# A score tile of four banks with one merge, and fold steps spread, in a kernel of window attention, a Fourier mix and a feed-forward layer

## The chip, the cores and the metric

The kernel runs on one core of a Trainium2 chip, and the metric is the device time of one execution in microseconds (us). The core has five engines that each work off their own queue in order: TensorE (PE, matmuls and transpositions; its weight loads stand in the profile as PEld), VectorE (DVE), ScalarE (ACT), GpSimd (POOL) and SyncE (SP, which here only issues transfers). They meet through semaphores. Matmuls write to PSUM, which has eight banks of 512 fp32 values per partition; the other working memory is SBUF.

## The reference

Attention for 4 batches, 8 heads, 768 positions and a head dimension of 64, with a window of 128 keys and 4 sink keys, then a Fourier mix with a feed-forward layer on the joined heads (width 512, hidden width 2048), all in fp32:

```python
scores = scale * np.matmul(q, k.transpose(0, 1, 3, 2))
keep = is_sink | in_window
scores = np.where(keep, scores, -1000000000.0)
scores = scores - np.max(scores, axis=-1, keepdims=True)
a = np.exp(scores)
a = a / (np.sum(a, axis=-1, keepdims=True) + 1e-09)
x = np.matmul(a, v)                      # then heads side by side: (4, 768, 512)
mixed = np.real(np.fft.fft(np.fft.fft(x, axis=1), axis=2))
u = x + mixed
un = (u - mean(u)) / np.sqrt(var(u) + 1e-06)
out = u + np.maximum(un @ w_ch1, 0.0) @ w_ch2
```

## The kernel before

**Blocks and steps.** Attention works through 24 blocks of 128 queries (4 batches of 6 blocks, numbered 0 to 23 below). A block has four steps, one for each pair of heads; step `s` is block `s // 4`, pair `s % 4`. The order of the instructions is written out by hand: for every step the lists in `SCHEDULE` say in which order ScalarE, VectorE, GpSimd and TensorE get their operations, and this order is kept up to step 97. An operation that belongs to a pair is issued some steps later than its scores (`STEP_LAG`), one that belongs to a block at a step counted from the block's first (`BLOCK_AT`). At an even step `scores` (L694) is called for two pairs, this one and the next: in what follows these four heads are a run, and a block has a first and a second run.

**Scores.** For each head `scores` puts 260 columns into one bank of a tile `s` of two banks (one pair of heads): 128 scores against the older key block, 4 against the sink keys, 128 against the newer block. The pool `ps_s` has two such tiles (L640), so four banks in all; the first pair of a run takes the one, the second the other. In the first block of a batch (blocks 0, 6, 12, 18) there is no older key block, and only 132 columns are written (L700).

**Merge and softs.** Each row needs only 128 of the 256 window scores, some from the older block and some from the newer. `merge` (L704) copies the older block's where the mask `older` says so, over the newer block's, for the two heads of a tile (L708, 128x256). `soft1` (L710) then does, for each head, one VectorE instruction that scales, adds the mask, writes 132 values to SBUF and keeps the row's extreme (L720), followed by a short read of the accumulator. `expo` (L723) is ScalarE's exponential.

**The sink strip.** `trans_sink` (L805, matmul L809) transposes the small sink weights of the block two before. It has no PSUM of its own for that: it writes into columns 384 to 511 of the second bank of the tile that holds the second pair of the current block (`st["free", g + 2, 1][:, 1, 384:]`). It is issued at the block's first step, on TensorE's queue, and `copy_sink` (L812, L814) takes it out with ScalarE at the second step, ahead of the exponentials of that step.

In program order, at the first step of block `g`, VectorE has `merge` and `soft1` of the first pair; then TensorE has the weighted sums of an earlier block (`av`, L789), `trans_sink`, the transpositions of exponentials (`trans_p`, L751), the Fourier matmuls if any (events `T`), and `turn_x` (L801, L803). At the second step ScalarE has `copy_sink`, and VectorE the merge and softs of the second pair, then `store_x` (L819). At the third and fourth step come the second run's. `inverse` (L742, L743) is at the fourth.

**Fourier transform.** `fourier` (L332) is called for a batch when its fourth block has been stored; it registers events by step and engine with `at`. For each of three pairs of 128-row tiles `j` (at `FOLD_AT` = 0, 4, 8 steps): `fold_n` (L351) adds and subtracts mirrored tiles, the sum on VectorE and the difference on GpSimd (`FOLD_ENG`), `fold_m` folds the columns (L361 on VectorE, L358 on GpSimd), `fold_hi` rounds on ScalarE (L364) and `fold_lo` keeps the rest on VectorE (L367). `put_row` (L380), `mid_sum` (L371) and `mid_row` (L375, L377) treat one odd row on VectorE. Then come the matmuls of the transform on TensorE (L394, L421, L442), their rounding on ScalarE (L401, L430) and VectorE (L409, L447, L448) and the update of `u` (L458, L459). The transforms of batches 0 to 2 in the order of work run beside the attention of the next batch; that of the last (`tail`) runs after it, beside the feed-forward layer's first group, and has all its folds on VectorE. The steps are constants:

```python
F_N, F_M, F_S, ROW = (3, 3), (4, 5), (6, 7), (5, 8, 10)
```

**Feed-forward.** From about 203 us weights are converted on VectorE (L590 to L592), split on ScalarE and GpSimd, and used in matmuls L619 and L1124, which fill TensorE to the end.

Of the kernel before, what the change touches and what calls it, by code (L numbers as in the profile page):

```python
# [11 lines left out]
F32 = mybir.dt.float32  # L12
# [7 lines left out]
P = 128  # L20
# [40 lines left out]
FILL_AT, FILL = (24, 36), 0  # L61
FOLD_AT, FOLD_LAST, FOLD_ENG = (0, 4, 8), (0, 4, 8), "VG"

F_N, F_M, F_S, ROW = (3, 3), (4, 5), (6, 7), (5, 8, 10)
EV_A = 0

SINK0_AT = 3, 3, "V"
# [138 lines left out]
def kernel(  # L206
# [63 lines left out]
    def run(general):  # L270
        tag = "g" if general else ""
        with ExitStack() as p1:
# [8 lines left out]
            def at(s, eng, fn):  # L281
                ev.setdefault((s, eng), []).append(fn)
# [49 lines left out]
            def fourier(b, at, ready):  # L332
# [15 lines left out]
                def fold_n(eng, j, odd):  # L348
                    t = fw.tile([P, DM], F32, tag=f"f{odd}", name=f"f{odd}_{b}_{j}", bufs=2 - odd)
                    t_["eo", j, odd] = t  # L350
                    eng.tensor_tensor(t, u[j], u[NHALF + j], op=ALU.subtract if odd else ALU.add)  # L351
# [11 lines left out]
                def fold_hi(j):  # L363
                    A.copy(gh[:, j], t_["g", j])  # L364

                def fold_lo(j):
                    V.tensor_tensor(gl[:, j], t_.pop(("g", j)), f32(gh[:, j]), op=ALU.subtract)  # L367
# [2 lines left out]
                    r = t_["x0"]  # L370
                    V.tensor_tensor(r[:, 1:256], r[:, 1:256], r[:, 511:256:-1], op=ALU.add)  # L371

                def mid_row():
                    t = t_["x0"]
                    V.tensor_copy(sph[:NR, :257], t[:, :257])  # L375
                    lo = sph[NR - 1:NR, :257]
                    V.tensor_tensor(lo, t[NR - 1:NR, :257], f32(lo), op=ALU.subtract)  # L377

# [85 lines left out]
                at(1, "S", load_row)  # L464
                for j in range(NHALF):
                    k = ready[j]
                    e0, e1 = FOLD_TAIL if tail else FOLD_ENG
                    eng = {"V": V, "G": G}
                    at(k + F_N[0], e0, lambda j=j: fold_n(eng[e0], j, 0))
                    at(k + F_N[1], e1, lambda j=j: fold_n(eng[e1], j, 1))  # L470
                    at(k + F_M[0], e0, lambda j=j: fold_m(eng[e0], j, 0))
                    at(k + F_M[1], e1, lambda j=j: fold_m(eng[e1], j, 1))
                    at(k + F_S[0], "A", lambda j=j: fold_hi(j))
                    at(k + F_S[1], "V", lambda j=j: fold_lo(j))
# [160 lines left out]
            def window_attention(fourier, load_constants):  # L635
                with ExitStack() as pa:
                    kpool = pa.enter_context(tc.tile_pool(name="kpool", bufs=1, side="right"))
                    aw = pa.enter_context(tc.tile_pool(name="aw", bufs=2, side="right"))
                    pb = ExitStack()
                    ps_s = pb.enter_context(tc.tile_pool(name="ps_s", bufs=2, space=PSUM))  # L640
                    ps_t = pa.enter_context(tc.tile_pool(name="ps_t", bufs=1, space=PSUM, side="right"))
                    ring = ring_.rearrange("p (h s w) -> p h s w", h=NP, s=NSLOT)
                    ident_r = kpool.tile([P, P], F32R, name="ident_r")
# [48 lines left out]
                        return bass.AP(a.tensor, a.offset, [list(a.ap[0]), [(r1 - r0) * W - 2, 2], [1, W - 2]])  # L692

                    def scores(g, hp):  # L694
                        st["s", g, hp] = st["free", g, hp] = ps = ps_s.tile([P, 2, 512], F32, tag="s", name=f"s_{g}_{hp}")
                        for j in range(2):
                            rows = slice(D * j, D * j + D)
                            if g % NB == 0:
                                q, k = st["whole", g]
                                T.matmul(ps[:, j, P:P + W], q[rows, hp, :], k[rows, hp, :W], start=True, stop=True)  # L700
                            else:
                                T.matmul(ps[:, j, :P + W], st["q", g][rows, hp, :], keys(g, 2 * hp + j), start=True, stop=True)  # L702

                    def merge(g, hp):  # L704
                        ps = st["s", g, hp]
                        qi = g % NB
                        if qi > 0:
                            V.copy_predicated(ps[:, :, P + NS:P + W], older[qi > 2], ps[:, :, 0:P])  # L708

                    def soft1(g, hp):  # L710
# [116 lines left out]
                    with ExitStack() as man:  # L827
# [52 lines left out]
                        V.scalar_tensor_tensor(mask[0][:, 0:1], sdist[:, 0:1], win_ap, nosink[:, 0:1], op0=ALU.is_ge, op1=ALU.mult)  # L880
                        def other_masks():
                            for i, op in enumerate((ALU.is_gt, ALU.is_lt)):
                                V.tensor_scalar(older[i], dist[:, None, :].broadcast_to([P, 2, P]), 0.0, None, op0=op)
# [453 lines left out]
```

## Time and profile before

| what | us |
|---|---|
| median of 3 runs | 786.71 (786.69 to 786.85) |
| the profiled execution | 786.78 |
| its span on the core | 784.9 |
| TensorE busy in the span | 755.2 |
| VectorE busy in the span | 460.6 |
| ScalarE, GpSimd busy | 239.0, 177.6 |

A row of the timeline has the start and the duration in us, engine, line, operation, output and inputs by the program's names, shapes and count, and in brackets how long the engine was idle before it and what ended the wait. A row of the waits has who waited for whom, total, times and longest. A row of groups has line, engine, operation, operands, count, busy time, mean duration in ns, and idle time before with what ended it. A row of stretches has its limits, its length, the busy time of TensorE, its weight loads, VectorE, ScalarE and GpSimd with their counts, TensorE's granted clock, the share of the transfer engines and GB/s.

### The profile page before, as it was taken

The numbers are of one execution on the slowest core, as the hardware profiler recorded it, in microseconds if no ns is written. First come the engines' busy times: TensorE is split into PE (matmuls) and PEld (weight loads), VectorE is DVE, ScalarE is ACT, GpSimd is POOL, SyncE is SP. The second block draws the span as 40 slices with busy tenths as digits, with TensorE's granted clock in tenths as the row PEclk, the third lists the DMA queues.
The fourth block names the chain that finished last, engine by engine and source line by source line (L and its number), as shares of the span: only waits on it lengthen the run. The fifth ranks groups of instructions, "written<-read, shape, count | busy, mean of one in ns | idle before, by whom it ended". The sixth has DMA issues, their size and how long they took to land.

```text
span 784.9 us, 11953 instructions
## 1 busy us (share of the span) xinstructions
PE 755.2 (96%) x4379; PEld 615.8 (78%) x4379; DVE 460.6 (59%) x1354; ACT 239.0 (30%) x704; POOL 177.6 (23%) x283
## 2 busy tenths in 40 slices
PE   7999998988899999999999999999999999999996
PEld 5666876866778878899888888888888888888895
DVE  6788687999999589561356424662456425611211
ACT  4887765756633133221111111111111110110110
POOL 2566477476645255200000000000000000000000
PEclk9999999999999999999999999999999999999999
DMA  9853525433305366120100002000200001000100
GB/s 311 251 171 109 140 84 176 127 112 99 131 27 159 111 196 210 62 71 1 54 1 0 1 9 99 1 1 0 81 1 0 1 0 54 1 1 0 55 1 32
DMA packets 41812, 57.69 MB, mean 74 GB/s; under 512 B 2796, under 2 KB 27500, under 8 KB 41360
## 3 DMA queue, kind: packets, MB, share of 16 engines
q1 hardware_dynamic: 41456, 53.07, 21.7%
q0 software_dynamic: 288, 3.76, 1.2%
q8 instruction: 37, 0.61, 0.3%
q14 instruction: 31, 0.25, 0.1%
HBM read 47.37 MB, written 9.45 MB: 72 GB/s over the span
## 4 chain that ended last, share of the span: by engine, by line
PE 80%; DVE 13%; issue 2%; POOL 1%; ACT 1%; DMA 1%; SPq 0%; DVEq 0%; ACTq 0%; POOLq 0%
PE h L619 33%; PE o L1124 33%; PE xt L789 3%; PE s L702 3%; DVE sm L720 2%; PE pt L751 2%; DVE cv L591 1%; PE za L394 1%; DVE s L708 1%; DVE cv L590 1%; PE a L421 1%; DVE cv L592 1%; DVE f L351 1%; PE x L801 1%; DMA vt<-in_v_sink_dram 1%
## 5 line engine op out<-in xcount | busy, mean ns | idle before, releaser
L1124 PE MATMUL o<-w,h 128*128 128x512 f32 x876 | 216.5, 394 | 0.0
L1117 DVE SCALAR_TENSOR_TENSOR h<-h,h 128x512 fp32r<-128x512 f32 (+1 forms) x107 | 65.4, 611 | 247.7 <-ACT h L1112 247.5
L1124 PEld LDWEIGHTS o<-w,h 128*128 128x128 f32 x876 | 162.8, 188 | 35.5
L1112 ACT ACTIVATE h<-h 128x512 fp32r<-128x512 f32 (+1 forms) x107 | 57.2, 535 | 366.4 <-PE h L619 360.1
L619 PE MATMUL h<-un_slots,w 128*128 128x512 f32 (+1 forms) x576 | 124.7, 365 | 0.0
L619 PEld LDWEIGHTS h<-un_slots,w 128*128 128x128 f32 x576 | 99.6, 188 | 19.6
L619 PE MATMUL h<-un_last,w 128*128 128x512 f32 (+1 forms) x432 | 89.0, 355 | 0.0
L619 PEld LDWEIGHTS h<-un_last,w 128*128 128x128 f32 x432 | 72.7, 188 | 12.8
L726 ACT ACTIVATE sm<-sm,mx 128x132 f32<-128x132 f32 x192 | 75.8, 400 | 7.1 <-DVE mx L720 7.1
L1148 DVE STREAM_TRANSPOSE unf<-un 32x128 f32<-32x128 f32 x224 | 67.7, 302 | 3.2
L702 PE MATMUL s<-ring,q 64*128 64x260 f32 x320 | 51.2, 422 | 12.2 <-DVE mx L720 6.4
L720 DVE CUSTOM_DVE_ANT_0 sm<-s,mask 128x132 f32<-128x132 f32 x192 | 48.7, 292 | 9.3 <-ACT skt L814 2.7
L702 PEld LDWEIGHTS s<-ring,q 64*128 64x128 f32 x320 | 27.1, 188 | 28.2 <-issue 12.4
L608 POOL TENSOR_TENSOR w<-cv,w 128x512 fp32r<-128x512 f32 x25 | 33.9, 1354 | 35.5 <-ACT w L607 35.4
L789 PE MATMUL xt<-ptl,ldv 128*64 128x128 f32 x384 | 38.9, 288 | 0.0
L708 DVE COPY_PREDICATED s<-older,s 128x256 f32<-128x256 uint8 x80 | 33.6, 420 | 7.2 <-ACT skt L814 6.8
L726 ACT ACTIVATION_READ_ACCUMULATOR sm<-sm,mx 128x1 f32 x192 | 36.8, 192 | 0.0
L1124 PE MATMUL o<-w_ring,h 128*128 128x512 f32 x144 | 35.6, 393 | 0.0
L767 POOL TENSOR_SCALAR_AFFINE_SELECT ptl<-pta 128x512 f32<-128x512 f32 x48 | 32.2, 672 | 14.4 <-ACT pta L758 14.4
L789 PEld LDWEIGHTS xt<-ptl,ldv 128*64 128x64 f32 x384 | 21.6, 137 | 14.9 <-issue 8.1
L789 PE MATMUL xt<-pta,ldv 128*64 128x128 f32 x320 | 31.7, 277 | 0.2 <-POOL pta L775 0.2
L751 PE MATMUL pt<-ident,sm 128*128 128x128 f32 x192 | 31.6, 288 | 0.0
(200 smaller groups left out, 1040.9 us busy)
## 6 DMA issues: line engine op xcount, KB each, us to landing
raw<-in_moe_w_ch_dram SPq DMA_DIRECT2D x32, 512.0 KB, 3.7
ldv<-in_v_dram SPq DMA_DIRECT2D x28, 256.0 KB, 3.6
ring<-in_qk_dram SPq DMA_DIRECT2D x24, 264.0 KB, 4.6
out_dram<-u SPq DMA_DIRECT2D x24, 256.0 KB, 3.8
q<-in_qk_dram SPq DMA_DIRECT2D x20, 256.0 KB, 4.2
cst<-in_dft_dram POOLq DMA_DIRECT2D x1, 3348.0 KB, 11.7
ud<-us SPq DMA_DIRECT2D x12, 256.0 KB, 2.2
u<-ud SPq DMA_DIRECT2D x2, 1024.0 KB, 5.1
```

The source lines that it names most:

```text
L608: G.tensor_tensor(d[1], tf, f32(d[0]), op=ALU.subtract)
L619: T.matmul(ps[:, :tb], a[:, cs], x[:, :, cc, :], start=n == 0, stop=n == 3 * NCC - 1)
L702: T.matmul(ps[:, j, :P + W], st["q", g][rows, hp, :], keys(g, 2 * hp + j), start=True, stop=True)
L708: V.copy_predicated(ps[:, :, P + NS:P + W], older[qi > 2], ps[:, :, 0:P])
L720: V.tensor_tensor_reduce(sm[:, h % 4], ps[:, j, P:P + W], mask[min(qi, 3)], -SCALE, 3.0e38, ALU.add, ALU.min, accum_out=mx[:, 0, h:h + 1])
L726: A.activation(sm[:, h % 4], sm[:, h % 4], AF.Exp, bias=mx[:, 0, h:h + 1], scale=-1.0, accum_out=mx[:, 1, h:h + 1])
L751: T.transpose(ps[:, j], sm[:, j, NS:], ident)
L789: T.matmul(ps[D * j:D * j + D, p, :], st["v", kb(g) - i][:, h, :], a[:, h % 4, :], start=i == 0, stop=i == n - 1)
L1112: A.activation(h[0], ps[:, :tb], AF.Relu)
L1117: V.scalar_tensor_tensor(h[1], ps[:, :tb], 0.0, f32(h[0]), op0=ALU.max, op1=ALU.subtract)
L1124: T.matmul(po[i], a[:, ts_], x, start=f == 0 and n == 0, stop=f == NF - 1 and n == 2)
L1148: V.transpose(unf[32 * q:32 * q + 32, :, r], un[r].rearrange("p (c q j) -> p c q j", c=NCC, q=4)[:, :, q])
```

## The change

Two edits. First, `ps_s` holds one tile of four banks instead of two of two. The four heads of a run share it: it is taken at even pairs, and each pair's `soft1` reads its half. `merge` is done once for a run, 128x512, at the run's first pair, and the masks `older` are twice as wide. `trans_sink` still writes into the last bank of the second pair's half, which is now bank 3 of the common tile; its place in the order is the same.

Second, the fold steps get two sets. For the first three transforms' first and second tile pair the difference on GpSimd moves one step later, its column fold one step later, `fold_hi` and `fold_lo` one step later; for the third tile pair, and the whole last transform, only the difference moves by one step. `mid_row` becomes two events: the copy `mid_hi` on ScalarE at step 9, and `mid_lo` on VectorE at step 13 (both were on VectorE at step 10).

```diff
-F_N, F_M, F_S, ROW = (3, 3), (4, 5), (6, 7), (5, 8, 10)
+F_STEPS = ((3, 4), (4, 5), (6, 7)), ((3, 4), (4, 6), (7, 8))
+ROW = 5, 8, 9, 13
...
-                def mid_row():
+                def mid_hi():
+                    A.copy(sph[:NR, :257], t_["x0"][:, :257])
+
+                def mid_lo():
                     t = t_["x0"]
-                    V.tensor_copy(sph[:NR, :257], t[:, :257])
                     lo = sph[NR - 1:NR, :257]
                     V.tensor_tensor(lo, t[NR - 1:NR, :257], f32(lo), op=ALU.subtract)
...
                 for j in range(NHALF):
                     k = ready[j]
+                    f_n, f_m, f_s = F_STEPS[0 if tail or j == NHALF - 1 else 1]
...
-                at(ready[0] + ROW[2], "V", mid_row)
+                at(ready[0] + ROW[2], "A", mid_hi)
+                at(ready[0] + ROW[3], "V", mid_lo)
...
-                    ps_s = pb.enter_context(tc.tile_pool(name="ps_s", bufs=2, space=PSUM))
+                    ps_s = pb.enter_context(tc.tile_pool(name="ps_s", bufs=1, space=PSUM))
...
                     def scores(g, hp):
-                        st["s", g, hp] = st["free", g, hp] = ps = ps_s.tile([P, 2, 512], F32, tag="s", name=f"s_{g}_{hp}")
+                        if hp % 2 == 0:
+                            st["four"] = ps_s.tile([P, 4, 512], F32, tag="s", name=f"s_{g}_{hp}")
+                        st["s", g, hp] = st["free", g, hp] = ps = st["four"][:, 2 * (hp % 2):2 * (hp % 2) + 2]
+                        st["four", g, hp] = st["four"]
...
                     def merge(g, hp):
-                        ps = st["s", g, hp]
+
+                        ps = st.pop(("four", g, hp))
                         qi = g % NB
-                        if qi > 0:
+                        if qi > 0 and hp % 2 == 0:
                             V.copy_predicated(ps[:, :, P + NS:P + W], older[qi > 2], ps[:, :, 0:P])
...
-                        older = [kpool.tile([P, 2, P], U8, name=f"older{i}") for i in range(2)]
+                        older = [kpool.tile([P, 4, P], U8, name=f"older{i}") for i in range(2)]
...
-                                V.tensor_scalar(older[i], dist[:, None, :].broadcast_to([P, 2, P]), 0.0, None, op0=op)
+                                V.tensor_scalar(older[i], dist[:, None, :].broadcast_to([P, 4, P]), 0.0, None, op0=op)
```

More of the change, by code (lines that the diff above doesn't have):

```diff
@@ L466, in fourier @@
                     k = ready[j]
+                    f_n, f_m, f_s = F_STEPS[0 if tail or j == NHALF - 1 else 1]
                     e0, e1 = FOLD_TAIL if tail else FOLD_ENG
                     eng = {"V": V, "G": G}
[L469 to L474, printed above, removed]
+                    at(k + f_n[0], e0, lambda j=j: fold_n(eng[e0], j, 0))
+                    at(k + f_n[1], e1, lambda j=j: fold_n(eng[e1], j, 1))
+                    at(k + f_m[0], e0, lambda j=j: fold_m(eng[e0], j, 0))
+                    at(k + f_m[1], e1, lambda j=j: fold_m(eng[e1], j, 1))
+                    at(k + f_s[0], "A", lambda j=j: fold_hi(j))
+                    at(k + f_s[1], "V", lambda j=j: fold_lo(j))
                 at(ready[0] + ROW[0], "V", put_row)
                 at(ready[0] + ROW[1], "V", mid_sum)
-                at(ready[0] + ROW[2], "V", mid_row)
+                at(ready[0] + ROW[2], "A", mid_hi)
+                at(ready[0] + ROW[3], "V", mid_lo)
                 k = ready[2] + S1
```

## The prediction

> **What bounds the kernel now.** The page first, for the span; then the span cut into stages, because the engines change roles.
>
> ```profile
> span 784.9 us, 11953 instructions
> ```
>
> ```profile
> 23.00:48.00 25.00, 24.72 (x253) 18.06 (x251) 19.21 (x103) 20.94 (x84) 13.75 (x33) 1.00 0.79 233
> ...
> 78.00:104.00 26.00, 26.00 (x240) 21.57 (x240) 16.58 (x74) 18.23 (x67) 12.04 (x26) 1.00 0.42 115
> ...
> 144.00:203.00 59.00, 52.70 (x465) 41.39 (x463) 55.27 (x203) 38.21 (x139) 38.10 (x66) 1.00 0.36 111
> 203.00:260.00 57.00, 51.91 (x312) 44.14 (x310) 55.87 (x90) 21.94 (x49) 31.41 (x27) 0.97 0.34 106
> 260.00:785.00 525.00, 517.74 (x2455) 429.56 (x2453) 237.19 (x567) 80.76 (x148) 27.77 (x25) 1.00 0.11 37
> ```
>
> Columns of the stages: stretch, length, busy time of PE, PEld, VectorE (DVE), ACT, POOL. The change works up to about 203 us, in the 24 blocks of attention. In 23 to 48 and 78 to 104 PE is full; in 144 to 260 VectorE is. After 260 PE is full and nothing is changed. Since VectorE stays full from 144 to 260, what attention loses or gains by 203 us is passed on to the end; that is the quantity I compute.
>
> Who waits on whom (20 to 205 us; total, times, longest):
>
> ```profile
> DVE s L708 <- ACT skt L814: 6.8, 11, 1.3
> ...
> DVE sm L720 <- ACT skt L814: 2.7, 2, 1.6
> ```
>
> VectorE loses 9.5 us to ScalarE's copy of the sink strip. The place, in block 6 and then all of block 7 (16 score matmuls per block, 8 records for a pair of head pairs):
>
> ```profile
> 45.22 0.29 DVE L720 CUSTOM_DVE_ANT_0 sm<-s,mask 128x132 f32<-128x132 f32 x1 [1.58 <-ACT skt L814]
> ...
> 47.92 1.15 PE L702 MATMUL s<-ring,q 64*128 64x260 f32 x8
> ...
> 50.02 0.28 PE L809 MATMUL s<-ident_r,sk 128*128 128x128 f32 x1
> ...
> 50.34 0.27 ACT L814 CAST skt<-s 128x128 fp32r<-128x128 f32 x1
> ...
> 50.64 0.43 DVE L708 COPY_PREDICATED s<-older,s 128x256 f32<-128x256 uint8 x1 [0.49 <-ACT skt L814]
> ...
> 51.36 1.15 PE L702 MATMUL s<-ring,q 64*128 64x260 f32 x8
> ```
>
> The row at 45.22 decides my forecast. That instruction reads bank 0 of its score tile; what it waited 1.58 us for is a copy out of bank 1, columns 384 on, of the same tile. So a wait covers the whole score tile, not the bank. A tile of four banks then couples more: the transposition of the sink strip (L809), written into the four-bank tile after the first head pair's softs in program order, must wait for those softs, and the second head pair's softs for the copy.
>
> **The change, part by part.** Prices, from these rows:
>
> ```profile
> 54.59 0.29 DVE L720 CUSTOM_DVE_ANT_0 sm<-s,mask 128x132 f32<-128x132 f32 x1
> 54.80 0.08 DVE L720 DVE_READ_ACCUMULATOR2_ANT mx<- 128x1 f32 x1
> ```
>
> ```profile
> 55.00 0.33 PEld L702 LDWEIGHTS s<-ring,q 64*128 64x128 f32 x4 [0.59 <-PE s L702]
> ```
>
> ```profile
> 96.10 1.15 PE L702 MATMUL s<-ring,q 64*128 64x260 f32 x8
> ...
> 96.86 0.43 DVE L708 COPY_PREDICATED s<-older,s 128x256 f32<-128x256 uint8 x1 [0.47 <-PE s L702]
> ```
>
> ```profile
> L819 DVE TENSOR_TENSOR us<-x,mx 128x512 f32<-128x512 f32 x9 | 6.2, 685 | 1.4 <-PE x L803 1.4
> ...
> L361 DVE TENSOR_TENSOR f<-f 128x255 f32<-128x255 f32 x9 | 5.3, 592 | 0.0
> ...
> L883 DVE TENSOR_SCALAR older<-scratch 128x256 uint8<-128x256 f32 x2 | 0.5, 296 | 0.0
> ```
>
> - Last soft to next scores: 54.88 to 55.00, 0.12 us. Today only the second half of a run waits for it; with one buffer the whole run does.
> - Scores to merge: at 96.10 a merge of half the run began 0.76 us after the scores' start. Half a run ends near 0.71, a whole one at 1.15, so a merge of all four banks begins at 1.20.
> - The merge of 128x512 is not in the trace. Bounds: 0.43, as at 96.86 (width free), and 0.86 (two of today's). I take 0.69, by L819, which reads 128x512 from PSUM in 685 ns; with the step to the next instruction 0.75. 40 of 80 merges go.
> - Softs: 0.22 from start to start and 0.08 at the end (54.59, 54.80, ended 54.88), so 0.51 for two heads and 0.94 for four.
> - Transposition to free softs: 50.02 to 50.64, 0.62.
>
> First run of a block, from its scores: merge at 1.20, two softs done 2.46, transposition 2.58 (today 50.02 less 47.92, 2.10), softs freed 3.20, last soft 3.71. PE needs 1.34 from the transposition to the next scores (50.02 to 51.36), so these come at 3.92; today 3.44. Second run: 1.20 + 0.75 + 0.94 + 0.12 = 3.01; today 2.75:
>
> ```profile
> 23.21 1.20 PE L702 MATMUL s<-ring,q 64*128 64x260 f32 x8
> ...
> 54.11 0.71 PE L702 MATMUL s<-ring,q 64*128 64x260 f32 x4
> ...
> 68.58 0.71 PE L702 MATMUL s<-ring,q 64*128 64x260 f32 x4
> ```
>
> A light block takes 6.93. Today blocks 3 to 6 take 24.71 (23.21 to 47.92), 6.18 each. **Blocks 1 to 5 and 7: 6 x 0.75 = +4.5 us.** The two `older` masks double in width at the start, before the first merge: at most 2 x 0.30, I take **+0.5**. Block 6, without a merge: 0.
>
> What queues behind the new waits: on PE, behind the transposition, the transpositions of the exponentials and the turn of the block before; on VectorE, behind the second softs, the fold's steps; on ScalarE, behind the copy, the exponentials of the pair before, which PE needs only a run later.
>
> **Blocks 8 and 9** (14.47 today, 54.11 to 68.58).
>
> ```profile
> 48.52 0.64 DVE L351 TENSOR_TENSOR f<-u 128x512 f32<-128x512 f32 x1
> ```
>
> ```profile
> 55.18 0.69 DVE L367 TENSOR_TENSOR gl<-f,gh 128x512 fp32r<-128x512 f32 x1
> ```
>  The spread fold steps put the fold's low part (L367) behind the first run. VectorE's gap before the first merge falls under the 1.32 that PE needs anyway (0.12 + 1.20); the gap before the second holds fold (0.59), low part (0.69), store (0.69) and a row step, which I estimate at 0.35: 2.3. Block: 3.71 + 2.3 + 0.75 + 0.94 + 0.12 = 7.82; two, 15.64: **+1.2**.
>
> **Blocks 10 to 13** are PE's (26.00 of 26.00). The transposition there stands 2.52 after the scores; 2.58 after the change: **+0.2**.
>
> **Blocks 14 and 15.** GpSimd's odd fold moves one step on, past its own selects; the cast of the middle row goes to ScalarE (38.21 of 59.00 busy: hidden). Here the folds' own edit pays:
>
> ```profile
> 106.52 1.51 DVE L367 TENSOR_TENSOR gl<-f,gh 128x512 fp32r<-128x512 f32 x1
> 107.96 1.12 DVE L351 TENSOR_TENSOR f<-us,us 128x512 f32<-128x512 f32 x1
> ...
> 115.00 0.65 DVE L375 CAST sph<-xr 33x257 fp32r<-33x257 f32 x1
> 115.69 0.74 DVE L377 TENSOR_TENSOR sph<-xr,sph 1x257 fp32r<-1x257 f32 x1
> ...
> 117.39 1.76 DVE L351 TENSOR_TENSOR f<-us,us 128x512 f32<-128x512 f32 x1
> ```
>
> ```profile
> 106.75 1.15 PE L702 MATMUL s<-ring,q 64*128 64x260 f32 x8 [1.15 <-DVE d L448]
> ...
> 124.90 1.15 PE L702 MATMUL s<-ring,q 64*128 64x260 f32 x8
> ```
>
> ```profile
> 116.90 1.70 POOL L351 TENSOR_TENSOR f<-us,us 128x512 f32<-128x512 f32 x1
> ```
>
> The 1.76 us fold ran beside GpSimd's own of 1.70; alone it took 0.64. Low parts, cast and row leave these gaps, so both first runs become PE's 1.32. In block 14 the second merge still follows two combinations that need PE: about 8.06. Block 15: 3.71 + 2.2 + 1.69 + 0.12 = 7.72. Together 15.8 against 18.15 today; as GpSimd's updates may hold block 16, I take **-2.1**. The Trainium skill (SBUF — State Buffer, Who interferes with whom) says that a VectorE instruction with two SBUF inputs contends with a GpSimd one that reads SBUF; by that rule the spread only moves the crowding onto the next fold step, and the trace's 1.76 agrees with the rule; the term would then be about -1.
>
> **Blocks 16, 17, 22 and 23.** A merge held by late inputs now holds PE's transposition too:
>
> ```profile
> 134.62 1.15 PE L702 MATMUL s<-ring,q 64*128 64x260 f32 x8
> 137.14 0.30 PE L809 MATMUL s<-ident_r,sk 128*128 128x128 f32 x1
> ```
>
> ```profile
> 136.54 0.41 DVE L708 COPY_PREDICATED s<-older,s 128x256 f32<-128x256 uint8 x1
> ```
>
> Merge at 1.92, so transposition at 1.92 + 0.75 + 0.51 + 0.12 = 3.30, not 2.52: +0.8 in block 17; I take 16, 22 and 23 as like it: **+3.3**. The block's Fourier matmuls queue behind it.
>
> **Blocks 18 to 21** are VectorE's: first run 0.75 + 0.51 + 0.12 + 0.62 + 0.51 = 2.51 against some 1.97 today (two merges and four softs), second 1.69: +0.26 a block, +1.0; casts to ScalarE and uncrowded folds -1.5: **-0.5**. The last transform's cast, on the full VectorE after 203, leaves it too: **-0.6**.
>
> Sum: 4.5 + 0.5 + 1.2 + 0.2 - 2.1 + 3.3 - 0.5 - 0.6 = **+6.5**. The profiled execution took 786.78, its span 784.9, the median is 786.71: **793**.
>
> **The rivals.**
> *VectorE's sum decides (faster).* From block 14 on, if every gap on VectorE holds more than 1.32 us and no merge starts late, only its work counts: 18 runs with 0.28 less (1.97 to 1.69) 5.0, crowded folds about 4, casts 1.2, the tail 0.6, against +6.4 up to block 13: 786.8 + 6.4 - 10.8 = **782**. For it: 55.27 of 59.00 busy. Against: the merges that start late for their inputs, as at 136.54.
> *Waits by bank (faster).* If a wait covers banks, the transposition needs the merge alone (1.20 + 0.69 + 0.12 = 2.01, before PE is there) and only one soft needs the copy: a light block pays 0.26, VectorE's blocks gain 0.45 or more: 0.5 + 1.6 - 0.2 - 3.0 - 3.3 - 0.6 - 0.6 = -5.6: **781**. The Trainium skill (PSUM — Partial Sum Buffer, PSUM bank collisions raise a hardware error) asks for guards by bank and quadrant. The row at 45.22 speaks against it here.
> *The coupling compounds (slower).* Where the merge comes after the transposition today, as in block 15 (119.07 against 116.91), PE would stall 119.07 + 1.38 - 116.91 = 3.5 us:
>
> ```profile
> 116.91 0.30 PE L809 MATMUL s<-ident_r,sk 128*128 128x128 f32 x1
> ```
>
> ```profile
> 119.07 0.41 DVE L708 COPY_PREDICATED s<-older,s 128x256 f32<-128x256 uint8 x1
> ```
>
> If the folds' spread does not thin these gaps (the change does not do what it says), -2.1 and -0.5 fall away and block 15 adds 3.5: 786.8 + 9.1 + 3.5, about **799**.
>
> **How the numbers follow.** Forecast 0.56 (own range 789 to 798: the merge's bounds move it by -0.27 or +0.15 on some 20 runs that are on the path, -5 or +3, part hidden); VectorE's sum 0.17; by bank 0.08; compounding 0.19. A measurement of this kernel tells 0.2%, 1.6 us, from no change. Faster 0.25 (both rivals), same 0.07 (the forecast's low edge), slower 0.68. The range 781 to 800 leaves out the lower halves of the two faster rivals and a tail above the slower one, about 2 in 10.
>
> **What would show it.** Right: the transposition L809 in block 7 some 2.6 us after its scores and waiting for softs; score runs that never start before the last soft; the 128x512 merge near 0.69; light blocks near 6.9; folds on VectorE near 0.64. Wrong: L809 at 2.1 and light blocks at 6.2 to 6.4 (by bank), a merge near 0.42, or VectorE's idle time unchanged at the sink copy.

## The result, and the profile after

The changed kernel is slower, as forecast, and by more than forecast:

| | median, us | ratio to before (95% interval) |
|---|---|---|
| before, beside it | 786.78 (4 runs) | 1 |
| changed | 797.96 (796.64 to 800.87, 4 runs) | 1.0144 (1.0126 to 1.0162) |
| forecast | 793, range 781 to 800 | 1.008 |
| changed, once more beside other kernels | 799.06 (797.82 to 800.33, 4 runs) | 1.0156 (1.0132 to 1.0179) |

The page and the stages of the changed kernel (stretch, length, busy PE, PEld, VectorE, ScalarE, GpSimd, then the granted clock):

```profile
span 799.1 us, 11889 instructions
```

```profile
114.00:157.00 43.00, 37.53 (x286) 29.89 (x286) 31.74 (x113) 23.00 (x87) 23.80 (x44) 0.88 0.42 129
157.00:216.00 59.00, 51.14 (x454) 40.51 (x455) 49.14 (x186) 37.88 (x138) 37.85 (x65) 1.00 0.36 110
```

Attention now ends near 216 us, not 203. In the 59 us up to that end VectorE was busy for 55.27 before and is for 49.14 now: it waits more. This execution took 800.87 us and ran at a clock of 0.88 from 114 to 157 us; the second profiled one (span 796.1) ran there at 0.96:

```profile
114.00:157.00 43.00, 37.32 (x312) 28.99 (x312) 34.18 (x127) 24.55 (x92) 24.87 (x46) 0.96 0.46 139
```

Who waits on whom in the first of the two, 20 to 216 us (total, times, longest), and the group of the new merge:

```profile
DVE sm L730 <- ACT skt L824: 16.6, 21, 1.3
...
PE s L819 <- DVE mx L730: 8.9, 14, 1.7
```

```profile
L718 DVE COPY_PREDICATED s<-older,s 128x512 f32<-128x512 uint8 x40 | 27.6, 690 | 7.9 <-PE s L711 7.7
```

VectorE's waits for the copy of the sink strip grew from 9.5 to 16.6 us, and now it is the softs that wait (before it was mostly the second merge). New is the other row: TensorE's transposition of the strip (L819) waits for softs. Block 4, a light one, shows the whole loop (scores L711, merge L718, softs L730, copy L824):

```profile
33.08 1.15 PE L711 MATMUL s<-ring,q 64*128 64x260 f32 x8 [0.33 <-PE pt L761]
...
35.68 0.28 PE L819 MATMUL s<-ident_r,sk 128*128 128x128 f32 x1 [0.43 <-DVE mx L730]
...
37.02 1.15 PE L711 MATMUL s<-ring,q 64*128 64x260 f32 x8
...
40.11 0.49 PE L711 MATMUL s<-ring,q 64*128 64x260 f32 x2 [0.33 <-PE pt L761]
```

```profile
34.27 0.70 DVE L718 COPY_PREDICATED s<-older,s 128x512 f32<-128x512 uint8 x1 [0.76 <-PE s L711]
35.11 0.29 DVE L730 CUSTOM_DVE_ANT_0 sm<-s,mask 128x132 f32<-128x132 f32 x1
...
35.54 0.08 DVE L730 DVE_READ_ACCUMULATOR2_ANT mx<- 128x1 f32 x1
36.30 0.30 DVE L730 CUSTOM_DVE_ANT_0 sm<-s,mask 128x132 f32<-128x132 f32 x1 [0.67 <-ACT skt L824]
```

Merge 1.19 after the scores, transposition 2.60 after them and 0.06 behind the end of the first pair's softs (35.62), the second pair's softs 0.62 after the transposition (36.30), the next scores 3.94 after the first: forecast were 1.20, 2.58, 0.62 and 3.92. The block takes 7.03 (33.08 to 40.11; forecast 6.93, before 6.29).

What each stage adds to the time of before, from the first score matmul of every block in the traces, and the clock that TensorE was granted there:

| blocks | forecast | first execution | second execution | clock: before, first, second |
|---|---|---|---|---|
| up to 7, with the masks | +5.0 | +6.5 | +6.2 | 0.97, 1.00, 1.00 |
| 8, 9 | +1.2 | +1.0 | +1.0 | 1.00, 1.00, 1.00 |
| 10 to 13 | +0.2 | +0.7 | 0.0 | 1.00, 1.00, 1.00 |
| 14, 15 | -2.1 | +0.8 | -0.1 | 0.91, 0.90, 1.00 |
| 16, 17 | +1.6 | +3.8 | +2.6 | 1.00, 0.86, 0.92 |
| 18 to 21 | -0.5 | +0.1 | +0.1 | 1.00, 1.00, 1.00 |
| 22, 23 | +1.7 | +0.5 | +2.2 | 1.00, 1.00, 0.93 |
| after the last soft | -0.6 | +0.8 | -0.7 | |
| sum | +6.5 | +14.2 | +11.2 | |

The sums of the executions are the differences of their spans to 784.9. The clock is not low throughout a stage: it is halved for stretches of some 3.4 us, which lie at other places in each execution. One is in block 15 of before, one in block 16 of the second execution:

```profile
121.40:124.80 3.40, 3.40 (x24) 2.29 (x20) 2.48 (x13) 0.83 (x3) 3.23 (x8) 0.50 0.00 0
```

```profile
133.00:136.40 3.40, 3.31 (x23) 2.44 (x22) 2.89 (x8) 0.00 (x0) 1.43 (x3) 0.51 1.05 405
```

Another is in block 22 of the second execution (197.9 to 201.3); the first has one in block 14 (from 116.3) and two running in block 16 (133.4 to 140.2). Where TensorE is busy throughout, such a stretch can cost half its length, 1.7 us by this estimate, so a single stage of a single execution is known no better than that. I use the second column of measurements, and say where the clock matters.

### The profile page after: what moved, and what is told of

It is laid out like the page before. It is cut to its first block, busy times and chain, and to the rows that moved or that the text cites. A ratio compares the mean times of both kernels' runs of the same rounds, so it can differ in the third digit from the quotient of the medians.

```text
span 799.1 us, 11889 instructions
## 1 busy us (share of the span) xinstructions
PE 757.2 (95%) x4379; PEld 621.8 (78%) x4379; DVE 452.3 (57%) x1310; ACT 239.8 (30%) x708; POOL 180.3 (23%) x283
## 4 chain that ended last, share of the span: by engine, by line
PE 79%; DVE 13%; issue 3%; ACT 2%; POOL 1%; DMA 1%; SPq 0%; DVEq 0%; ACTq 0%; POOLq 0%
PE o L1134 32%; PE h L625 31%; PE s L711 4%; PE xt L799 3%; DVE sm L730 2%; PE pt L761 2%; DVE s L718 1%; PE za L398 1%; DVE cv L598 1%; DVE cv L597 1%; PE a L425 1%; PE x L811 1%; DVE cv L596 1%; ACT sm L736 1%; PE zr L398 1%
## 5 line engine op out<-in xcount | busy, mean ns | idle before, releaser
L711 PE MATMUL s<-ring,q 64*128 64x260 f32 x320 | 46.9, 410 | 16.2 <-issue 9.1
L730 DVE CUSTOM_DVE_ANT_0 sm<-s,mask 128x132 f32<-128x132 f32 x192 | 47.0, 292 | 24.4 <-ACT skt L824 16.6
L711 PEld LDWEIGHTS s<-ring,q 64*128 64x128 f32 x320 | 29.2, 188 | 26.1 <-issue 16.4
L614 POOL TENSOR_TENSOR w<-cv,w 128x512 fp32r<-128x512 f32 x25 | 36.8, 1474 | 33.6 <-ACT w L613 33.4
L718 DVE COPY_PREDICATED s<-older,s 128x512 f32<-128x512 uint8 x40 | 27.6, 690 | 7.9 <-PE s L711 7.7
L761 PE MATMUL pt<-ident,sm 128*128 128x128 f32 x192 | 31.5, 288 | 0.0
```

The source lines that it names most:

```text
L614: G.tensor_tensor(d[1], tf, f32(d[0]), op=ALU.subtract)
L730: V.tensor_tensor_reduce(sm[:, h % 4], ps[:, j, P:P + W], mask[min(qi, 3)], -SCALE, 3.0e38, ALU.add, ALU.min, accum_out=mx[:, 0, h:h + 1])
L761: T.transpose(ps[:, j], sm[:, j, NS:], ident)
```

## The experiments

Twelve runs, all compared with the kernel before on the same chip; the second execution of the changed kernel was one of them:

> The changed kernel once more, beside the next three on one chip, for a second profiled execution: the first one ran at a clock of 0.88 from 114 to 157 us. Both theories: 797 to 798; if the granted clock is 1.00 in blocks 14 to 17, their loss there should be smaller than the 4.5 us of the first profile (shift of the first scores of block 18 against block 14), toward 2 to 3.

| label | what it is | median, us | ratio to before (interval) |
|---|---|---|---|
| e1 | before + spread fold steps alone | 787.32 | 1.0006 (0.9995 to 1.0018) |
| e2 | before + four-bank tile with one merge alone | 802.96 | 1.0195 (1.0181 to 1.0209) |
| e3 | changed, strip not transposed | 790.09 | 1.0038 (1.0018 to 1.0057) |
| e4 | before, strip not transposed | 785.95 | 0.9994 (0.9985 to 1.0003) |
| e5 | changed, a merge for each pair | 808.38 | 1.0273 (1.0259 to 1.0287) |
| e6 | before, transposition first on TensorE | 787.83 | 1.0003 (0.9988 to 1.0017) |
| e7 | changed, transposition in another bank | 800.57 | 1.0153 (1.0125 to 1.0182) |
| e10 | e1 + e6 | 789.40 | 1.0028 (1.0012 to 1.0044) |
| e12 | changed, transposition right behind the scores | 792.46 | 1.0072 (1.0054 to 1.0090) |
| e14 | e1, the fold's cast and low part later | 787.64 | 1.0005 (0.9993 to 1.0016) |
| e16 | e14 + transposition right behind the scores | 785.71 | 0.9991 (0.9979 to 1.0003) |

### The two edits apart: e1 and e2

e1 is the part of the diff with `F_STEPS`, `ROW`, `mid_hi` and `mid_lo`, on the kernel before; e2 is the rest of it.

> The kernel before with the folds' edit alone (fold steps in two sets, the middle row's cast on ScalarE); score tiles stay two of two banks. Theory A (the four-bank tile alone costs the time, the spread gains what the prediction said): the spread is worth about -2 to -4 (uncrowded folds -2, casts to ScalarE -0.6 or more), so 783 to 785. Rival (the spread only moves the crowding of VectorE and GpSimd onto the next fold step): 786 to 787, no change, with folds on VectorE of 1.1 us and more still in the blocks where two fold steps meet.

> The kernel before with the four-bank tile and the one merge alone; the fold steps stay as they were. Theory A: all of the loss is here, and as much more as the spread gains: the changed kernel's 797.5 plus 2 to 4, so 799 to 802. Rival (the spread is part of the loss, since it fills gaps that PE needs): below 797, toward 793.

All of the loss is in the tile (e2), and with two-bank tiles the spread is worth nothing in sum (e1). But with the four-bank tile it is worth 4 to 5 us (802.96 against 797.96 and 799.06). So the two edits are not terms to be added.

The rival's reason for e1 is only in part what the trace shows. The column folds did not get shorter (592 ns before, 612 in e1), but the low parts on VectorE in the three transforms beside attention did (groups of 44 to 200 us, busy, mean in ns; first before, then e1):

```profile
L367 DVE TENSOR_TENSOR gl<-f,gh 128x512 fp32r<-128x512 f32 x9 | 8.4, 937 | 0.3 <-ACT gh L364 0.3
```

```profile
L369 DVE TENSOR_TENSOR gl<-f,gh 128x512 fp32r<-128x512 f32 x9 | 6.8, 760 | 0.0
```

Much of what VectorE gained it spent waiting: its waits for the copy of the strip rose from 9.5 to 14.5 us (11.8 and 2.7 in the waits of e1). In block 9 of e1 it reached the second pair's merge earlier and stood there until the sink strip was copied, where before it waited only for its own work:

```profile
66.48 0.43 DVE L714 COPY_PREDICATED s<-older,s 128x256 f32<-128x256 uint8 x1 [1.21 <-ACT skt L820]
```

By first scores, e1's nothing is a loss and a gain: it is 2.0 us behind before at block 10, still 1.2 at block 18, and 0.8 ahead at block 22.

e2 shows why the same spread pays on the shared tile. In block 20 a low part and a fold hold the merge back, and the transposition on TensorE (L813 there) has to wait for the softs behind that merge:

```profile
176.34 0.68 DVE L367 TENSOR_TENSOR gl<-f,gh 128x512 fp32r<-128x512 f32 x1
176.94 1.12 DVE L351 TENSOR_TENSOR f<-u 128x512 f32<-128x512 f32 x1
177.99 0.68 DVE L712 COPY_PREDICATED s<-older,s 128x512 f32<-128x512 uint8 x1
```

```profile
179.28 0.28 PE L813 MATMUL s<-ident_r,sk 128*128 128x128 f32 x1 [1.97 <-DVE mx L724]
```

```profile
PE s L813 <- DVE mx L724: 17.9, 18, 2.0
```

17.9 us of such waits in e2, 8.9 in the changed kernel. On the shared tile a first merge that VectorE reaches late holds TensorE's queue as soon as the transposition stands at its head; with two tiles the transposition does not wait for softs in any block.

### Is it the sink strip in the score tile? e3, e4, e7, e12

e3 and e4 (the same edit on the kernel before):

```diff
-                        T.transpose(ps, st.pop(("sk", g)).rearrange("p g h s -> p (g h s)"), ident_r)
-                        st["pk", g] = ps
+                        st["pk", g] = st.pop(("sk", g)).rearrange("p g h s -> p (g h s)")
```

> The changed kernel without TensorE's transposition of the sink weights into the score tile: ScalarE's copy takes the small strip straight from SBUF instead, untransposed. It leaves out that transposition, so the output's part from the sink keys is not computed as in the reference; all other work stays. Theory A (the wait covers the whole tile, so the transposition has to wait for the first pair's softs and the second pair's softs for the copy): these waits are nearly the whole loss, so 786 to 788, 10 to 12 below the changed kernel; VectorE's waits for the copy (16.6 us in 21 waits) gone. Rival (one buffer: the whole run of scores waits for the last soft, whatever the transposition does): 3 below the changed kernel at most, 794 to 795.

> The kernel before with the same left out (the sink weights are not transposed, and the sink keys' part of the output is not the reference's). Theory A: VectorE's 9.5 us of waits for the copy lie partly in time in which it waits for PE anyway; 1 to 3 below before, 784 to 786, and the gap to the changed kernel with the same left out shrinks from 11 to 1 to 3. Rival (one buffer alone): the gap between the two stays at 8 or more.

Without the transposition the changed kernel is 8 to 9 us faster; the kernel before gains less than can be told. So 7 to 8 of the 11 to 12 us hang on the strip. Theory A's 786 to 788 for e3 was missed, and the gap that is left between e3 and e4 is 4.1 us, above its 1 to 3 and well below the rival's 8: the coupling is two thirds of the loss, and the single buffer, the one merge, the wider masks and the spread together are the rest. In e3 the copy is gone from VectorE's waits, and TensorE's scores end the largest part of them:

```profile
DVE s L718 <- PE s L711: 11.1, 15, 2.2
```

A light block of e3 takes 6.48 us (first scores of blocks 4 and 5, 32.70 and 39.18), 0.55 less than in the changed kernel.

e3 leaves work out as well as a wait, so two kernels keep the work. e12 issues the transposition directly behind the block's first scores, into the same place:

```diff
                                 lag(scores, s, -1)
+                                if k == 0 and 2 <= g < NQ:
+                                    trans_sink(g - 2)
...
+                                        if op == "trans_sink" and at_ // NP + 2 < NQ:
+                                            continue
```

> The changed kernel with one thing moved: the transposition of the sink strip is issued directly behind the block's first scores, ahead of merge and softs in program order, into the same bank 3 of the same four-bank tile. All work is done. Now only the merge has to wait for the transposition, and the softs and ScalarE's copy only read the tile. Theory A (the coupling between transposition, softs and copy through the tile is most of the loss): near the kernel without the transposition (790.1), with the merge 0.1 to 0.3 later in 20 blocks: 790 to 793; a light block near 6.5 where the changed kernel takes 7.03. Rival (leaving the transposition out gained by the work it saved): 796 or more, a light block near 7.

By the time, 792.46, theory A: about 6 us come back by a move in program order alone, and the saved work was not the reason. The light block, though, went only to 6.96 (expected 6.5), as the rival had it. Up to block 8 e12 has gained nothing on the changed kernel (6.8 us behind before, with a half-clock stretch from 16.3 to 23.1; second execution 6.2), and it gains only from block 17 on: at block 23 it is 6.5 behind, the second execution 12.0, of which up to 1.7 is the half-clock stretch in block 22. So the move pays where the first merge comes late, and hardly in the light blocks. Block 4 of e12 shows what stayed there, from VectorE, ScalarE and TensorE, and then the waits from 20 to 216 us:

```profile
35.04 0.69 DVE L718 COPY_PREDICATED s<-older,s 128x512 f32<-128x512 uint8 x1 [0.96 <-PE s L819]
...
36.32 0.08 DVE L730 DVE_READ_ACCUMULATOR2_ANT mx<- 128x1 f32 x1
36.79 0.29 DVE L730 CUSTOM_DVE_ANT_0 sm<-s,mask 128x132 f32<-128x132 f32 x1 [0.39 <-ACT skt L824]
```

```profile
36.49 0.27 ACT L824 CAST skt<-s 128x128 fp32r<-128x128 f32 x1 [0.74 <-PE pt L761]
```

```profile
35.96 0.66 PE L761 MATMUL pt<-ident,sm 128*128 128x128 f32 x4
```

```profile
ACT skt L824 <- DVE mx L730: 26.9, 14, 3.4
...
DVE sm L730 <- ACT skt L824: 9.9, 21, 1.1
```

I expected the copy and the softs, which only read the tile, to run side by side. They do not: the copy out of bank 3 begins 0.09 us after the first pair's softs out of banks 0 and 1 end (36.40), the second pair's softs 0.03 us after the copy ends (36.76), and the waits name both directions. The row names TensorE's L761 for the copy, but that ended at 36.62, after the copy's start. The same 0.09 stands in 18 of the 22 blocks with a strip, the 0.03 in all 22. In this program engines take turns at a score tile, readers too. The Trainium skill (PSUM — Partial Sum Buffer, PSUM bank collisions raise a hardware error) asks for guards by bank and quadrant; here the wait spans banks, so it is wider than that rule needs. Narrowing it was not tried.

e7 takes the strip out of the score tile altogether, into the bank of the weighted sums (`xt`), where that is free:

```diff
-    "copy_sink": 9,
+    "copy_sink": 12,
-    "trans_sink": 8,
+    "trans_sink": 11,
...
-                        ps = (st["free", g + 2, 1][:, 1, 384:].bitcast(F32R) if g + 2 < NQ else
-                              ps_t.tile([P, P], F32R, tag="pt", name=f"pk_{g}"))
+                        ps = ps_t.tile([P, P], F32R, tag="xt", name=f"pk_{g}")
```

> The changed kernel with the sink strip's transposition taken out of the score tile: it goes into the bank of the weighted sums' tile at the step in which that is free (three steps later, its copy one step after it). All work is done. Theory A (the coupling through the score tile is most of the loss): about as without the transposition (790.1) plus its time on PE and a wait for the copy of the weighted sums, together 0.3 to 0.5 in the blocks where PE sets the pace: 790 to 793. Rival (leaving the transposition out gained by the work it saved, 24 x 0.28 us on PE and as much on ScalarE's path): 795 or more.

By its time this is a miss for theory A (800.57). By its trace the strip has changed its partner. Up to block 9 it gains: first scores 5.4 us behind before, 6.5 in the second execution of the changed kernel. Then it loses, at block 15 12.3 behind against 8.4. TensorE just ahead of block 4, where it pays, and in block 14, where it does not; then ScalarE there:

```profile
31.52 0.28 PE L818 MATMUL pk<-ident_r,sk 128*128 128x128 f32 x1 [0.16 <-ACT xs L804]
```

```profile
117.07 1.12 PE L799 MATMUL xt<-ptl,ldv 128*64 128x128 f32 x8 [1.53 <-POOL ptl L777]
```

```profile
116.19 0.62 ACT L366 CAST gh<-f 128x512 fp32r<-128x512 f32 x1 [2.90 <-POOL f L360]
```

The strip's copy now has to leave the bank before the next weighted sums, and ScalarE works it off behind a cast that waited 2.90 us for GpSimd; the weighted sums wait for GpSimd too. But the clock was halved there from 116.3 to 123.1 us, and TensorE was busy for 9.90 us in block 14 where the second execution of the changed kernel needed 7.28: of the 3.6 us by which the block is longer, 2.6 are that. What the waits cost beside the clock was not separated, so e7 shows that another shared bank brings waits of its own, and does not decide between theory A and its rival.

### What the one merge is worth: e5

```diff
-                        ps = st.pop(("four", g, hp))
+                        ps = st["s", g, hp]
...
-                        if qi > 0 and hp % 2 == 0:
-                            V.copy_predicated(ps[:, :, P + NS:P + W], older[qi > 2], ps[:, :, 0:P])
+                        if qi > 0:
+                            V.copy_predicated(ps[:, :, P + NS:P + W], older[qi > 2][:, :2], ps[:, :, 0:P])
```

> The changed kernel (four-bank tile, spread) with a merge for each pair again, 128x256 each, so that the first pair's softs start after half the copying. Theory (the one merge pays by itself, 0.69 against twice 0.42 and the steps between, and the shared tile loses): a run's work on VectorE grows by 0.3 or so, the transposition comes 0.3 earlier and the second pair's end 0.2 to 0.3 later; 1 to 4 above the changed kernel, 799 to 802. Rival (the long merge is what holds the transposition, and with it PE, so that halves are better on a shared tile): 794 to 797, the gain in blocks 16 to 23, where the transposition waits longest.

808.38, some 10 us above the changed kernel: the theory's direction, and two and a half times the upper end of its size. Block 4 of e5, TensorE, then VectorE:

```profile
35.63 1.15 PE L711 MATMUL s<-ring,q 64*128 64x260 f32 x8 [0.64 <-PE pt L761]
...
37.96 0.28 PE L819 MATMUL s<-ident_r,sk 128*128 128x128 f32 x1 [0.16 <-DVE mx L730]
...
39.70 1.15 PE L711 MATMUL s<-ring,q 64*128 64x260 f32 x8 [0.33 <-DVE scratch L936]
```

```profile
38.57 0.43 DVE L718 COPY_PREDICATED s<-older,s 128x256 f32<-128x256 uint8 x1 [0.67 <-ACT skt L824]
```

The transposition came 0.27 us earlier (2.33 after the scores, not 2.60), the wait for the copy stayed at 0.67, and the second merge now stands behind that wait; the next scores came after 4.07, not 3.94. A light block took 7.47 (35.63 to 43.10), 0.44 more than 7.03. I had counted the gain and the loss against each other; on a tile with one user at a time nothing runs beside the second merge here, so all of it counts. Not all of the time is that, though: in the profiled executions e5 is 11.2 us longer than the second one of the changed kernel, 6.2 of them ahead of block 22 (up to 3.4 of these by a half-clock stretch from 17.1 to 24.0), and the other 5 in blocks 22 and 23 and after attention, where its granted clock was 0.87 and, for 20 us, 0.83 (0.93 and 1.00 in the changed kernel). So where the tile is shared the one merge gains some 3 to 6 us by these traces; the 9 to 10 between the medians hold the clock as well. The sharing costs more than either.

### Why the spread does not pay with two-bank tiles: e6, e10, e14, e16

e6, in both order lists for a block's first step:

```diff
-            ["av", "trans_sink", "T", "trans_p", "turn_x"],
+            ["trans_sink", "av", "T", "trans_p", "turn_x"],
...
-            ["av", "trans_p", "trans_sink", "T", "turn_x"],
+            ["trans_sink", "av", "trans_p", "T", "turn_x"],
```

> The kernel before with the transposition of the sink strip moved ahead of the weighted sums on TensorE's queue at a block's first step; nothing else. Theory A says VectorE's waits for the sink copy (9.5 us in all) shrink by the 0.6 to 1.1 us that the weighted sums take, but only part of them is on the path: 784.5 to 786. Rival (they are covered by waits for PE anyway, as leaving the transposition out altogether gained 1.0): 786 to 787, and the weighted sums that now come later may cost as much.

> The kernel before with the spread fold steps and with the transposition of the sink strip first on TensorE's queue; score tiles of two banks. Theory B: the spread alone gained nothing because, with the low part of the fold gone from the first step, VectorE reaches the second pair's merge earlier and waits there for the sink copy (1.21 us in block 9 of the spread-only kernel, where before there was no wait); with the copy earlier the spread pays, 783.5 to 785.5, 1.5 to 3 below the spread alone. Rival (the spread itself is worth nothing with two-bank tiles, the fold work only changes places): 786.5 to 787.5 as the spread alone.

e6 changed nothing: the rival. e10 was no better than e1, so theory B fell. The transposition came early, the copy did not. ScalarE, then VectorE, in block 9 of e10:

```profile
65.41 0.62 ACT L366 CAST gh<-f 128x512 fp32r<-128x512 f32 x1 [1.78 <-POOL f L360]
...
66.72 0.24 ACT L820 CAST skt<-s 128x128 fp32r<-128x128 f32 x1
```

```profile
67.00 0.43 DVE L714 COPY_PREDICATED s<-older,s 128x256 f32<-128x256 uint8 x1 [1.21 <-ACT skt L820]
```

The spread moved the fold's cast on ScalarE (`fold_hi`) by a step, and there it stands ahead of the strip's copy and waits for GpSimd's column fold, which the spread also made later. That gave theory C, and e14: e1 with

```diff
-F_STEPS = ((3, 4), (4, 5), (6, 7)), ((3, 4), (4, 6), (7, 8))
+F_STEPS = ((3, 4), (4, 5), (6, 7)), ((3, 4), (4, 6), (8, 10))
```

> The kernel before with the spread fold steps, two-bank tiles, and one thing more: ScalarE's cast of a fold moves one step further (8 instead of 7), behind the sink copy in ScalarE's order, and VectorE's low part to 10. Theory C (the spread put the cast, which waits for GpSimd's column fold, ahead of the sink copy on ScalarE; in block 9 of the run before this one the cast waited 1.78 us and took 0.62, and VectorE's second pair waited 1.21 for the copy): the 2.0 us that the spread lost from block 7 to 10 come back, 784.5 to 786. Rival (the spread only moves crowded work about): 786.5 to 788, blocks 7 to 10 still 1.5 to 2 later than before.

787.64, again no change, though the named wait is gone. Blocks 8 and 16 of e14, VectorE, then TensorE:

```profile
58.22 0.43 DVE L714 COPY_PREDICATED s<-older,s 128x256 f32<-128x256 uint8 x1
```

```profile
129.89 0.69 DVE L520 BATCH_NORM_STATS2 bn<-u 128x6 f32<-128x512 f32 x1 [2.39 <-POOL u L463]
...
130.71 0.98 DVE L369 TENSOR_TENSOR gl<-f,gh 128x512 fp32r<-128x512 f32 x1
131.61 0.42 DVE L714 COPY_PREDICATED s<-older,s 128x256 f32<-128x256 uint8 x1
```

```profile
131.75 0.44 PE L398 MATMUL za<-cst,gl 128*128 128x386 f32 x1 [1.04 <-DVE gl L369]
```

The second pair no longer waits in block 8, and block 9 starts 0.7 us behind before where e1 was 1.3 behind. But by block 10 it is 1.8 behind (e1 2.0), and in block 16 the later low part stands behind an operation that waits for GpSimd, and holds the merge and the transform's matmuls; block 17 starts 4.6 behind before (e1 1.2). Of the 4.3 us that block 16 of e14 loses, up to 1.7 go with a half-clock stretch (133.6 to 137.0); e16, at a clock of 1.00 there, still loses 2.7. Theory C is right about the place and wrong about its worth.

e16 adds the edit of e12 to e14:

> The kernel before with two-bank tiles, the spread with the later cast, and the transposition of the sink strip directly behind the block's first scores, so that neither a pair's softs nor its merge waits for the sink copy. Theory C with A: VectorE's 9.5 us of waits for the copy are gone and the spread pays: 783 to 785, below before. Rival (what VectorE gains it spends waiting for PE, as leaving the transposition out gained only 1): 786 to 787.

785.71, a ratio whose interval ends at 1.0003: at most a gain too small to be told. VectorE's 9.5 us of waits for the copy fell to 3.3 (2.0 and 1.3 in the waits of e16), as theory C with A says, but the time stays with the rival. None of these kernels is measurably faster than the one before.

## Why the prediction was right or wrong

**Right.** The direction, and what decided it. The reading of the row at 45.22, that a wait covers the whole score tile, holds: the transposition follows the softs out of other banks by 0.06 us in block 4, and e12 shows it from the other side. The prices hold: scores to merge 1.19 to 1.22 (1.20), the merge 0.690 (0.69, taken from a store of the same shape), transposition at 2.60 (2.58), first run 3.94 (3.92), light block 7.03 (6.93). The 0.1 of the light block is in the step from merge to first soft: 0.75 forecast, 0.84 measured (34.27 to 35.11). Blocks 8 to 13 came out within 0.3 in the second execution.

**Wrong in size, 793 for 798.** Five terms of the sum, by the second execution:

- *"Blocks 14 and 15: -2.1"* measured -0.1, the largest miss. (Before's 18.15 holds a half-clock stretch, the second execution's 18.02 none, so at equal clock the miss is larger still.) I expected both first runs on TensorE's 1.32 and 2.2 us of VectorE's work ahead of block 15's second merge. VectorE from block 15 into 16 (second execution), then GpSimd and ScalarE:

```profile
122.88 0.95 DVE L353 TENSOR_TENSOR f<-us,us 128x512 f32<-128x512 f32 x1
...
126.05 0.29 DVE L730 CUSTOM_DVE_ANT_0 sm<-s,mask 128x132 f32<-128x132 f32 x1 [0.94 <-ACT skt L824]
...
126.49 1.06 DVE L369 TENSOR_TENSOR gl<-f,gh 128x512 fp32r<-128x512 f32 x1
127.47 1.50 DVE L363 TENSOR_TENSOR f<-f 128x255 f32<-128x255 f32 x1
...
130.27 0.70 DVE L718 COPY_PREDICATED s<-older,s 128x512 f32<-128x512 uint8 x1
...
134.97 0.68 DVE L718 COPY_PREDICATED s<-older,s 128x512 f32<-128x512 uint8 x1
```

```profile
126.96 1.73 POOL L353 TENSOR_TENSOR f<-us,us 128x512 f32<-128x512 f32 x1
```

```profile
124.46 0.62 ACT L366 CAST gh<-f 128x512 fp32r<-128x512 f32 x1 [2.11 <-POOL f L360]
...
125.78 0.24 ACT L824 CAST skt<-s 128x128 fp32r<-128x128 f32 x1
```

  Between 126.49 and the merge at 130.27 lie 3.8 us of work. The sum on VectorE (L353) was partly freed, 0.95 where it had 1.76 (I expected 0.64), but GpSimd's difference, one step later, now lies on the column fold: 1.50, for which I took 0.59. The Trainium skill's rule that I weighed there (SBUF — State Buffer, Who interferes with whom) is that a VectorE instruction with two SBUF inputs contends with a GpSimd one that reads SBUF; the column fold is such an instruction, and its 1.50 beside GpSimd's 1.73 agrees with the rule. By it I had put the term at about -1, and set that aside.
- *"Blocks 16, 17, 22 and 23: +3.3"* measured 2.6 + 2.2, in part by the clock. In block 17 mechanism and price hold: transposition 3.31 after the scores (3.30), the block 0.8 longer. In block 16 (TensorE, second execution) the merge, at 134.97, came 2.92 and the transposition 4.21 us after the scores, where in block 16 of before it stood at 2.52: 1.7 for which I took 0.8.

```profile
132.05 1.17 PE L711 MATMUL s<-ring,q 64*128 64x260 f32 x8 [2.57 <-issue]
...
136.26 0.35 PE L819 MATMUL s<-ident_r,sk 128*128 128x128 f32 x1
```

  Yet the transposition's row names no wait: at half clock from 133.0 on, TensorE itself got there only when the softs ended (136.20). In e12, where the transposition waits for no softs, block 16 loses 1.7 too, with a half-clock stretch from 132.3 to 135.7. Late merge and slow clock lie on top of each other here, and no execution of the changed kernel shows block 16 without the second. In blocks 22 and 23 the first execution, at a clock of 1.00, lost 0.5, less than the 1.7 forecast; the second one's 2.2 hold the stretch in block 22.
- *"Blocks 1 to 5 and 7: 6 x 0.75"* with the masks: 6.2 for 5.0. By block 2 the kernel was 2.0 late, where masks and block 1 were to make 1.25. A late start is not the reason: e3 and e12 start block 1 0.0 and 0.2 late and are 2.1 and 1.9 behind at block 2, and kernels with two-bank tiles that start it 2.2 to 2.7 late (e6, e10, e14 and e16) are 0.3 to 0.9 behind there. The one tile is; I read this as scores that run ahead of the last softs on two tiles and cannot on one. Blocks 2 to 5 took 0.69 each, near 0.75 by two slips: 7.03 for 6.93, and the 6.18 of before has block 6 in it, which has no merge and takes 5.71 (blocks 3 to 5 take 6.33). Block 7 took 1.7, in e2 0.7. The moved difference crowds the column fold there as in block 15; it took 1.25, in e2 0.55 (second execution):

```profile
56.15 1.25 DVE L363 TENSOR_TENSOR f<-f 128x255 f32<-128x255 f32 x1
```

- *"Blocks 18 to 21: -0.5"* measured +0.1, near by luck: two misses of opposite sign. e2, without the spread, loses 3.7 there, at most 1.7 of it by a half-clock stretch (from 180.7), so the tile costs 2.0 to 3.7 for the forecast 1.0, and the spread gives back about as much for the forecast 1.5. With two-bank tiles, too, e1 gained 1.9 there.
- *A term at nothing.* I put the steps of ScalarE "behind the copy" and never costed the moved `fold_hi`, which is ahead of the copy. In block 15 (ScalarE's rows above) it waited 2.11 us for GpSimd, and VectorE's wait for the copy is 0.94, not 0.67.

**The rivals.** VectorE's sum (782): falsified, VectorE was not full any more (49.14 of 59.00). Waits by bank (781): falsified by 2.60 and 7.03. The compounding coupling (799): the nearest in time, and right in its mechanism, but near in time by luck. Its condition, that the spread does not thin the gaps, held in blocks 14 and 15 (-0.1, in e2 +0.2) and not in 18 to 21; and the 3.5 us that it put into block 15 did not come. The transposition's longest waits for softs in the second execution are in blocks 20 and 22, 1.0 and 1.8 us, with 0.2 in block 15. e2, where nothing is spread, costs 803. Between forecast and this rival I had drawn a line that the kernel does not have: both are one mechanism, by how late the merges come.

What stays open: how the 4.1 us between e3 and e4 split between the single buffer, the one merge, the masks and the spread, how much of blocks 16 and 22 is the clock's, and what e7 would take without its half-clock stretches.

## What to carry to other kernels

When users are put together on one buffer, list all of them, also one that borrows a corner of it, in program order: each hand-over becomes a serial step, an in-order queue behind it (here TensorE's, 8.9 us of waits) inherits delays of the other engine, and moving the borrower alone took back half of the loss (e12). Work taken off an engine pays only where that engine's lateness reaches the end: the same fold steps were worth nothing in sum on two tiles and 4 to 5 us on one. And a stage of two profiles can be compared only beside its granted clock: in block 16 a late merge and a half-clock stretch looked alike.

## What the runs showed that I had not expected

Two readers of one score tile wait for each other across banks: 9.9 us in 21 waits of e12, where no write stands between them. The merge of twice the width took 690 ns against 0.43 us for one of two, so joining two saves 0.17 us of their own time, but 0.44 us in a light block (7.03 against 7.47), where nothing runs beside it. And shorter instructions on VectorE, 760 for 937 ns on nine low parts, left the time of e1 where it was.
